# Separate PSUM banks and copies for the third x tile's transposes, and warm-up matmuls that read one broadcast column: a change to the first microseconds of an MLP forward and backward kernel

## The chip, the cores and the metric

The kernel runs on one core of one Trainium2 chip. The metric is the device time of one execution in microseconds (us). A profiled execution also has a span, from its first to its last traced instruction; for this kernel it is about 1.8 us shorter than the device time. Engines: PE is TensorE (PEld its weight loads), DVE is VectorE, ACT is ScalarE, POOL is GpSimd, SP is SyncE, which here only issues DMAs.

## The reference, cut to what matters

```python
def _fwd_reference(x, w1, w2):          # x [1, 2048, 640], w1 [640, 1536], w2 [1536, 640], bf16
    h = jax.nn.silu(jnp.einsum("bsd,df->bsf", x, w1))
    return jnp.einsum("bsf,fd->bsd", h, w2)

def reference(x, w1, w2, grad_out):     # the output and the three gradients
    _out, _vjp = jax.vjp(_fwd_reference, x, w1, w2)
    return (_out, *_vjp(grad_out))
```

These are six matrix products. The first product needs x with its 640 columns on partitions, that is, transposed. The rows are worked on in four chunks of 512.

## The kernel before: the opening

Only the opening of the first chunk is touched. TensorE is given 18 warm-up matmuls on a constant tile while the first inputs travel. Three x tiles of 128 rows are then transposed on TensorE, copied from PSUM to the tile `xT` by VectorE and ScalarE, and multiplied with w1, which comes in row blocks of 128 rows.

```python
NWARM = 18; NQ = 3; HC = NQ * P         # P = 128, DT = 640/128 = 5, FC = 512
NA = 8; FA = NA * P                     # eight output tiles are worked on at once
ps_h = tc.tile_pool(name="ps_h", bufs=8, space=PSUM)     # eight PSUM buffers, taken in turn
...
warm = cpool.tile([P, P], dt_in, name="warm")
early = [nc.vector.memset(warm[:], 1.0)]
wp = ps_h.tile([P, SC], FP32, name="wp", tag="hp")
for i in range(NWARM):
    early.append(nc.tensor.matmul(wp[:, 0:P], lhsT=warm[:], rhs=warm[:], start=True, stop=True))
...
early += [load_x(nc.sync, 0), load_x(nc.scalar, 1), load_x(nc.sync, 2)]
early += [load_w1(0, slice(0, FC), nc.scalar), load_w1(0, slice(FC, FA))]
early += [load_w1(k, slice(0, FA)) for k in range(1, 3)]
for k in range(3, DT):
    load_w1(k, slice(0, FA))
...                                     # later on the same queue: the rest of w1, then w2, ...
def pe_x(xT):
    slices = ((0, 1), (1, 3), (3, DT))
    tps = [ps_h.tile([P, hi - lo, NQ, P], dt_in, name="tp", tag="hp") for lo, hi in slices]
    for q in range(NQ):                 # x tile q
        for tp, (lo, hi) in zip(tps, slices):
            for dt_ in range(lo, hi):
                nc.tensor.transpose(
                    tp[:, dt_ - lo, q, :], x_nat[:, q, dt_ * P:(dt_ + 1) * P], ident[:])
    for k, (tp, (lo, hi)) in enumerate(zip(tps, slices)):
        copy_tp = nc.scalar.copy if k % 2 else nc.vector.tensor_copy
        copy_tp(out=xT[:, lo:hi, 0:HC], in_=tp[:].rearrange("p k q s -> p k (q s)"))

def h_first(xT, aT, ghT):
    pe_x(xT)
    ...
    for dt_ in range(DT):               # one row block of w1 after the other
        for ft in range(NA):
            mm(ft, dt_, slice(0, HC), dt_ == 0, False)   # 128x384 matmul on hs[ft]
    ...
```

Each PSUM tile `tp` holds columns of all three x tiles, so a copy can start only when the third tile has been transposed: in the profile before, the third tile's first transpose starts at 3.37 us and the first copy at 3.64.

## Time and profile before

| | before |
|---|---|
| device time, median of the 3 runs at hand (range) | 320.03 us (319.85 to 320.49) |
| span of the profiled execution | 317.7 us |
| PE busy | 313.2 us, 99% of the span |
| first matmul on w1's second row block | 5.60 us |

The profile's page gives the span, the busy time of each engine, and the chain of work that ended last, followed back from the last instruction.

```profile
span 317.7 us, 3605 instructions
...
PE 313.2 (99%) x1501; PEld 146.8 (46%) x1529; DVE 102.9 (32%) x182; ACT 77.2 (24%) x139; POOL 0.7 (0%) x6
...
PE 99%; issue 1%; DVE 0%; DVEq 0%
```

TensorE bounds the kernel. Time can be won only where TensorE waits or runs slowly, and that is the opening. The timeline of its first 6.3 us has the columns: start in us, duration of the merged group in us, engine, line, operation, tiles, shapes, count, and in brackets the idle time of the engine before it with what ended it.

```profile
0.29 0.17 DVE L158 MEMSET warm<- 128x128 bf16 x1 [0.29 <-issue]
...
0.51 2.10 PE L162 MATMUL wp<-warm 128*128 128x128 bf16 x18 [0.51 <-DVE warm L158]
...
2.43 1.39 PE L211 MATMUL tp<-ident,x_nat 128*128 128x128 bf16 x15
...
3.64 0.82 DVE L216 COPY xT<-tp 128x384 bf16<-128x384 bf16 x2 [3.19 <-PE tp L211]
...
3.75 0.80 ACT L216 COPY xT<-tp 128x768 bf16<-128x768 bf16 x1 [1.06 <-PE tp L211]
4.05 2.53 PE L251 MATMUL hp<-xT,w_nat 128*128 128x384 bf16 x13 [0.23 <-DVE xT L216]
...
4.86 0.44 PEld L251 LDWEIGHTS <-w_nat 128*128 128x128 bf16 x4 [0.39 <-DMA w_nat<-in_w_dram]
5.59 0.76 PEld L251 LDWEIGHTS <-w_nat 128*128 128x128 bf16 x6 [0.29 <-DMA w_nat<-in_w_dram]
```

Read from top to bottom: memset, 18 warm-ups, 15 transposes, copies, first h matmul at 4.05 us. The last two lines are weight loads that stood idle until a piece of w1 had landed. In the records of the single instructions the warm-ups are 105 to 108 ns apart (the first two 80), and so are the first transposes; from about 3.2 us the transposes are 55 to 57 ns apart, but for 62 and 66 where the third x tile arrives. Here this is called the clock of TensorE coming up, and the two paces half clock and full clock. The profile before has no record of the granted clock, so its moment is read from the spacing alone.

### The profile page before, as it was taken

The numbers are of one execution on the slowest core, as the hardware profiler recorded it, in microseconds if no ns is written. First come the engines' busy times: TensorE is split into PE (matmuls) and PEld (weight loads), VectorE is DVE, ScalarE is ACT, GpSimd is POOL, SyncE is SP. The second block draws the span as 40 slices with busy tenths as digits, with TensorE's granted clock in tenths as the row PEclk, the third lists the DMA queues.
The fourth block names the chain that finished last, engine by engine and source line by source line (L and its number), as shares of the span: only waits on it lengthen the run. The fifth ranks groups of instructions, "written<-read, shape, count | busy, mean of one in ns | idle before, by whom it ended". The sixth has DMA issues, their size and how long they took to land.

```text
span 317.7 us, 3605 instructions
## 1 busy us (share of the span) xinstructions
PE 313.2 (99%) x1501; PEld 146.8 (46%) x1529; DVE 102.9 (32%) x182; ACT 77.2 (24%) x139; POOL 0.7 (0%) x6
## 2 busy tenths in 40 slices
PE   9999999999999999999999999999999999999997
PEld 6644444444444444444444444444444444444444
DVE  1396631577310177700157741000000100001001
ACT  2592000654101354311064420111100001001110
POOL 0000000000000000000000000000000000000000
DMA  8989999999989885482644089919999999996011
GB/s 266 329 167 207 229 267 245 337 255 279 292 220 339 203 241 133 148 283 85 165 119 131 0 274 264 206 31 295 244 254 254 253 218 343 242 274 207 33 35 50
DMA packets 147264, 66.85 MB, mean 210 GB/s; under 512 B 113328, under 2 KB 146736, under 8 KB 147248
## 3 DMA queue, kind: packets, MB, share of 16 engines
q1 hardware_dynamic: 146960, 66.33, 82.0%
q10 hardware_dynamic: 288, 0.30, 0.3%
q8 instruction: 12, 0.20, 0.3%
q14 instruction: 4, 0.03, 0.0%
HBM read 9.18 MB, written 28.97 MB: 120 GB/s over the span
## 4 chain that ended last, share of the span: by engine, by line
PE 99%; issue 1%; DVE 0%; DVEq 0%
PE hp L299 32%; PE hp L283 16%; PE hp L388 16%; PE hp L439 15%; PE hp L220 13%; PE hp L251 3%; PE hp L419 1%; PE wp L162 1%; PE tp L211 0%; DVE xT L216 0%; DVE g L430 0%; DVE warm L158 0%; DVEq L430 0%; DVEq L467 0%
## 5 line engine op out<-in xcount | busy, mean ns | idle before, releaser
L283 PE MATMUL hp<-goT,w2T 128*128 128x512 bf16 x238 | 56.8, 380 | 0.1
L299 PE MATMUL hp<-aT,w_nat 128*128 128x512 bf16 x235 | 52.2, 379 | 0.3
L299 PE MATMUL hp<-ghT,w1T 128*128 128x512 bf16 x236 | 52.2, 379 | 0.2
L388 PE MATMUL hp<-a_blk,go_nat 128*128 128x512 bf16 x235 | 51.7, 379 | 0.3
L439 PE MATMUL hp<-gh_blk,x_nat 128*128 128x512 bf16 x220 | 48.3, 379 | 0.2
L220 PE MATMUL hp<-xT,w_nat 128*128 128x512 bf16 x192 | 47.8, 379 | 0.4
L307 ACT ACTIVATE oT<-hp 128x512 bf16<-128x512 f32 x24 | 14.4, 598 | 104.3 <-PE hp L299 104.3
L229 ACT ACTIVATE aT<-hp 128x512 bf16<-128x512 f32 x48 | 28.5, 614 | 37.2 <-PE hp L220 30.4
L283 PEld LDWEIGHTS <-w2T 128*128 128x128 bf16 x240 | 23.5, 98 | 28.3
L299 PEld LDWEIGHTS <-w_nat 128*128 128x128 bf16 x240 | 23.5, 98 | 28.3
L388 PEld LDWEIGHTS <-go_nat 128*128 128x128 bf16 x240 | 23.5, 98 | 28.3
L299 PEld LDWEIGHTS <-w1T 128*128 128x128 bf16 x240 | 23.4, 98 | 28.4
L290 DVE SCALAR_TENSOR_TENSOR ghT<-ghT,hp 128x512 bf16<-128x512 bf16 x48 | 32.5, 682 | 7.0 <-PE hp L283 7.0
L439 PEld LDWEIGHTS <-x_nat 128*128 128x128 bf16 x224 | 21.9, 98 | 26.5
L309 DVE CAST oT<-hp 128x512 bf16<-128x512 f32 x16 | 11.0, 690 | 70.6 <-PE hp L299 70.6
L236 DVE SCALAR_TENSOR_TENSOR ghT<-aT,v 128x512 bf16<-128x512 bf16 x48 | 32.6, 686 | 0.3
L220 PEld LDWEIGHTS <-w_nat 128*128 128x128 bf16 x200 | 19.5, 98 | 23.4
L235 DVE TENSOR_SCALAR v<-t 128x512 bf16<-128x512 f32 x48 | 20.1, 425 | 28.1 <-ACT t L233 28.1
L233 ACT ACTIVATE t<-hp 128x512 f32<-128x512 f32 x44 | 26.5, 620 | 0.0
L450 DVE CAST g<-hp 128x512 bf16<-128x512 f32 x7 | 4.8, 691 | 47.0 <-PE hp L439 28.2
L398 DVE CAST g2T<-hp 128x512 bf16<-128x512 f32 x7 | 4.8, 692 | 46.1 <-PE hp L388 46.1
L396 ACT ACTIVATE g2T<-hp 128x512 bf16<-128x512 f32 x8 | 4.8, 597 | 47.0 <-PE hp L388 47.0
(24 smaller groups left out, 42.0 us busy)
## 6 DMA issues: line engine op xcount, KB each, us to landing
aT_scr<-aT SPq DMA_DIRECT2D x4, 1536.0 KB, 6.2
ghT_scr<-ghT SPq DMA_DIRECT2D x4, 1536.0 KB, 8.0
out_dram<-o_sb SPq DMA_DIRECT2D x8, 640.0 KB, 3.7
oT_scr<-oT SPq DMA_DIRECT2D x4, 640.0 KB, 3.9
go_nat<-in_grad_out_dram SPq DMA_DIRECT2D x4, 640.0 KB, 7.7
gxT_scr<-oT SPq DMA_DIRECT2D x4, 640.0 KB, 5.2
w_nat<-in_w_dram SPq DMA_DIRECT2D x1, 1920.0 KB, 11.8
x_nat<-in_x_dram SPq DMA_DIRECT2D x3, 640.0 KB, 7.4
```

Source lines behind the costliest of these rows:

```text
L220: nc.tensor.matmul(hp[:], lhsT=w1_nat[:, dt_, ft * P:(ft + 1) * P], rhs=xT[:, dt_, :], start=(dt_ == 0), stop=(dt_ == DT - 1),)
L229: nc.scalar.activation(aT[:, ft, :], hp[:], ACT.Silu)
L233: nc.scalar.activation(t[:], hp[:], ACT.Tanh, scale=0.5)
L235: nc.vector.tensor_scalar(out=v[:], in0=t[:], scalar1=-0.5, scalar2=0.5, op0=ALU.mult, op1=ALU.add)
L236: nc.vector.scalar_tensor_tensor(out=ghT[:, ft, :], in0=aT[:, ft, :], scalar=1.0, in1=v[:], op0=ALU.subtract, op1=ALU.mult)
L283: nc.tensor.matmul(gp[:], lhsT=w2T[:, dt_, ft * P:(ft + 1) * P], rhs=goT[:, dt_, :], start=(dt_ == 0), stop=(dt_ == DT - 1),)
L290: nc.vector.scalar_tensor_tensor(out=ghT[:, ft, :], in0=ghT[:, ft, :], scalar=1.0, in1=gp[:], op0=ALU.add, op1=ALU.mult)
L299: nc.tensor.matmul(op_[:], lhsT=w_all[:, ft, dt_ * P:(dt_ + 1) * P], rhs=rhs_all[:, ft, :], start=(ft == 0), stop=(ft == FT - 1),)
L307: nc.scalar.activation(oT[:, dt_, :], op_[:], ACT.Copy)
L309: nc.vector.tensor_copy(out=oT[:, dt_, :], in_=op_[:])
L388: nc.tensor.matmul(gp[:], lhsT=go_nat[:, st, dt_ * P:(dt_ + 1) * P], rhs=a_blk[:, st, :], start=(st == 0), stop=(st == ST - 1),)
L439: nc.tensor.matmul(gp[:], lhsT=x_nat[:, st, dt_ * P:(dt_ + 1) * P], rhs=gh_blk[:, st, :], start=(st == 0), stop=(st == ST - 1),)
```

## The change

The intent is to start the first h matmuls earlier. The first two x tiles get PSUM banks of their own, so that their copies run while the third is still being transposed, and only a 128-column copy remains between the third tile's first transpose and the first h matmul. The warm-ups read one column of ones, repeated with step zero, so that the memset ahead of them shrinks from 128 columns to 2; a 19th warm-up fills the time won.

```diff
-    NWARM = 18
+    NWARM = 19
...
-        warm = cpool.tile([P, P], dt_in, name="warm")
+        warm = cpool.tile([P, 2], dt_in, name="warm")
+        warm_pp = warm[:, 0:1].to_broadcast([P, P])
...
-            early.append(nc.tensor.matmul(wp[:, 0:P], lhsT=warm[:], rhs=warm[:], start=True, stop=True))
+            early.append(nc.tensor.matmul(wp[:, 0:P], lhsT=warm_pp, rhs=warm_pp, start=True, stop=True))
...
         def pe_x(xT):
-            slices = ((0, 1), (1, 3), (3, DT))
-            tps = [ps_h.tile([P, hi - lo, NQ, P], dt_in, name="tp", tag="hp") for lo, hi in slices]
-            for q in range(NQ):
+            slices = ((0, 1), (1, DT))
+            for qs in ((0, 1), (2,)):
+                tps = [ps_h.tile([P, hi - lo, len(qs), P], dt_in, name="tp", tag="hp") for lo, hi in slices]
+                for k, q in enumerate(qs):
+                    for tp, (lo, hi) in zip(tps, slices):
+                        for dt_ in range(lo, hi):
+                            nc.tensor.transpose(
+                                tp[:, dt_ - lo, k, :], x_nat[:, q, dt_ * P:(dt_ + 1) * P], ident[:]
+                            )
                 for tp, (lo, hi) in zip(tps, slices):
-                    for dt_ in range(lo, hi):
-                        nc.tensor.transpose(
-                            tp[:, dt_ - lo, q, :], x_nat[:, q, dt_ * P:(dt_ + 1) * P], ident[:]
-                        )
-            for k, (tp, (lo, hi)) in enumerate(zip(tps, slices)):
-                copy_tp = nc.scalar.copy if k % 2 else nc.vector.tensor_copy
-                copy_tp(out=xT[:, lo:hi, 0:HC], in_=tp[:].rearrange("p k q s -> p k (q s)"))
+                    copy_tp = nc.scalar.copy if lo and len(qs) > 1 else nc.vector.tensor_copy
+                    copy_tp(
+                        out=xT[:, lo:hi, qs[0] * P:(qs[-1] + 1) * P], in_=tp[:].rearrange("p k q s -> p k (q s)")
+                    )
```

## The prediction

> **What bounds the kernel.** TensorE. Page: PE busy 313.2 of a 317.7 us span; chain of waits: 99% PE. From 5.60 us to the end the matmuls run back to back (longest start-to-start above the 216 ns pace: one of 431 ns at 13.5, about where a record is missing). Everything the change touches lies before 5.6 us, so the question is what ends last there.
>
> **The opening, from the timeline and the records of DMA landings.** The 128x128 memset runs 0.29 to 0.45 us (165 ns). Eighteen warm-up matmuls start at 0.51, 106 ns apart, the last at 2.29. Three x tiles land at 2.39, 2.82 and 3.33 us; each group of five transposes starts about 40 ns after its landing (2.43, 2.86, 3.37). So the transposes are bound by DMA, not by warm-ups. The third tile's first transpose releases the first VectorE copy (3.64, 358 ns for 384 columns); the first h matmul starts at 4.05. Four h matmuls run, then PE waits for w1's first row block, second half: landed 4.82, matmul 4.87 (weight load idle 0.39). After four more it waits for w1's second row block: landed 5.55, matmul 5.60 (idle 0.29). Later blocks land at 6.2, 6.85, 7.5, always ahead of their matmuls.
>
> **What the change does.**
> - Memset 64 times smaller: 165 ns to perhaps 60 to 100 (128x1 memsets on another engine take 99). Warm-ups start 0.07 to 0.1 us earlier; one more costs 106 ns; they end at about 2.40 as before, just as x lands.
> - Broadcast operands: I expect 106 ns spacing to stay. [...]
> - Separate copies: from VectorE's 358 ns (384 columns) and 549 ns (768), about 167 + 0.5 per column (estimate). The 256-column copy is done by about 3.6, before the third tile's first transpose ends; the 128-column copy takes about 230 ns instead of 358. First h matmul at about 3.92 instead of 4.05. ScalarE's copy grows from 768 to 1024 columns, about 1.0 us, but starts about 0.2 earlier: ends near 4.6 as before. VectorE's last copy (512 columns, about 420 ns) ends near 4.3.
> - Instruction order elsewhere is the same, except that the third xT load is issued after the first oT store; it is needed near 108 us, with tens of us to spare.
>
> **On the critical path.** The 0.13 us are gained ahead of two waits for w1 that do not move. The first eight h matmuls finish early and wait longer (idle 0.7 becomes about 0.85 us). The second row block's matmul still starts at about 5.6, so the gain is nearly zero.
>
> The clock is the other route: [...] spacing 106 ns until about 3.15 us and 56 ns after. [...] that too ends before 5.6 us.
>
> **Prediction.** 319.95 us, 80% range 319.4 to 320.6 (the range of before's three runs is 0.64 us). Chances: faster by over 2% 0.005, within 2% 0.985, slower 0.01.
>
> **Signs.** Right: first warm-up at 0.40 to 0.45; first h matmul at 3.85 to 3.95; weight load idle on w1 longer by about 0.13; second row block's matmul at 5.5 to 5.7; span 317.4 to 318.0. Wrong: PE idle on w1 shrinks, or that matmul starts before 5.45.
>
> **What would make it wrong.** Zero-step operands that run slower: 19 warm-ups at twice 106 ns would end near 4.4 and cost up to 1.5 us. A clock that comes up after 5.6 us. w1 landings that shift by chance; they set the start.

The forecast came to 319.95 us, 0.08 below the 320.03 of the three runs at hand; it does not split the 0.08. Cut from it, where marked, are what it said of broadcast operands and of the clock without a trace or run to show it, and with that one term, for the clock, to which it gave no figure. ScalarE's "about 1.0 us" for 1024 columns is an estimate; the profile before has 598 to 620 ns for its operations on 512 columns in PSUM and 798 for the copy of 768, which continue to 976 to 998.

## The result, and the profile after

| | before | after |
|---|---|---|
| median of 6 runs (range) | 320.16 us (319.72 to 320.63) | 320.09 us (319.36 to 320.52) |
| ratio of the means of the fast runs, 95% interval | | 0.9995 (0.9978 to 1.0011) |
| span of the profiled execution | 317.7 us | 317.8 us |
| first matmul on w1's second row block | 5.60 us | 5.75 us |

A ratio here is the mean time of one kernel's fast runs over the mean of the other's fast runs of the same rounds, so it is not quite the ratio of the medians.

The page after, with the chain's shares:

```profile
span 317.8 us, 3636 instructions
...
PE 315.1 (99%) x1530; PEld 147.6 (46%) x1530; DVE 102.9 (32%) x183; ACT 77.4 (24%) x139; POOL 0.7 (0%) x6
...
PE 98%; DMA 1%; DVE 0%; issue 0%; DVEq 0%; SPq 0%
```

PE's busy time and count differ by 1.9 us and 29 matmuls mostly because the trace before lacks some matmul records; 1530 matmuls are the whole program after, and 1529 before. So nothing may be read from that difference. The timeline of the opening, in the same columns as before:

```profile
0.25 0.06 DVE L159 MEMSET warm<- 128x2 bf16 x1 [0.25 <-issue]
...
0.38 2.21 PE L163 MATMUL wp<-warm 128*128 128x128 bf16 x19 [0.38 <-DVE warm L159]
...
2.67 1.52 PEld L213 LDWEIGHTS <-x_nat 128*128 128x128 bf16 x15 [0.35 <-DMA x_nat<-in_x_dram]
2.67 1.78 PE L213 MATMUL tp<-ident,x_nat 128*128 128x128 bf16 x15
...
3.53 0.29 DVE L218 COPY xT<-tp 128x256 bf16<-128x256 bf16 x1 [3.22 <-PE tp L213]
3.96 1.01 ACT L218 COPY xT<-tp 128x1024 bf16<-128x1024 bf16 x1 [1.27 <-PE tp L213]
4.07 0.23 DVE L218 COPY xT<-tp 128x128 bf16<-128x128 bf16 x1 [0.24 <-PE tp L213]
...
4.34 9.00 PE L255 MATMUL hp<-xT,w_nat 128*128 128x384 bf16 x80
```

The parts are as designed: the memset takes 0.06 us, the warm-ups start at 0.38 instead of 0.51, and a 128-column copy of 225 ns precedes the first h matmul. Yet that matmul starts at 4.34 us, later than before, and the h matmuls then run in one unbroken group; no line here waits for w1. Two things differ that the change did not aim at. The first x tile landed at 2.63 us instead of 2.39. And after the first pair (82 ns) the transposes are 106 to 107 ns apart to the last one: the record of the granted clock has it at full speed only from 4.59 us, where before it was up at about 3.2. The chain of waits for the first 6.2 us of each kernel (columns: start, duration, what) says the same:

```profile
...
0.51 2.10 PE wp L162 x18
2.61 1.01 PE tp L211 x11
3.62 0.02 issue
3.64 0.37 DVE xT L216
4.01 0.04 issue
4.05 0.81 PE hp L251 x4
4.86 0.01 issue
4.87 1.39 PE hp L251 x7
```

```profile
...
0.09 2.54 DMA x_nat<-in_x_dram
2.63 0.04 issue
2.67 1.78 PE tp L213 x15
4.46 1.78 PE hp L255 x10
```

The first fence is before, the second after. Before, the chain runs through the VectorE copy; after, from the landing of x through slow transposes straight into the h matmuls. (Before, four h matmuls take 0.81 us until the next starts at 4.87, where four at 0.16 us are 0.65: a wait for w1 lies in that piece.)

One sum holds for both; below it is called the identity. The span less the start of the first matmul on w1's second row block is 317.681 - 5.598 = 312.083 us before and 317.819 - 5.747 = 312.072 us after. All that differs between the two executions lies ahead of that matmul. Whether its start, 0.15 us later, is due to the change or to the execution is the question for the experiments.

### The profile page after: what moved, and what is told of

The parts are those of the page before. It is cut to its first block, busy times and chain, and to the rows that moved or that the text cites. A ratio compares the mean times of both kernels' runs of the same rounds, so it can differ in the third digit from the quotient of the medians.

```text
span 317.8 us, 3636 instructions
## 1 busy us (share of the span) xinstructions
PE 315.1 (99%) x1530; PEld 147.6 (46%) x1530; DVE 102.9 (32%) x183; ACT 77.4 (24%) x139; POOL 0.7 (0%) x6
## 4 chain that ended last, share of the span: by engine, by line
PE 98%; DMA 1%; DVE 0%; issue 0%; DVEq 0%; SPq 0%
PE hp L303 33%; PE hp L392 16%; PE hp L287 16%; PE hp L443 15%; PE hp L224 14%; PE hp L255 3%; PE hp L423 1%; DMA x_nat<-in_x_dram 1%; PE tp L213 1%; DVE g L434 0%; DVEq L434 0%; SPq L471 0%
```

## The experiments

Theory A is that of the prediction: the landing of w1's second row block sets the start of that matmul, so what is won earlier is lost in waiting. Theory B: the moment when the clock rises differs from execution to execution and sets the start. Theory C: the changed kernel itself makes the clock late, because broadcast operands count for less or because of the idle time before the first transpose.

All twelve profiles are put together here, with the two above. Times are us from the start of each span. "Copies" tells which form of the copies the kernel has. Landings are the last of the 16 completion records of a DMA. "Ended by" says "landing" where the second row block's first matmul starts within 0.05 us of that block's landing, and "pace" where the eight h matmuls before it took until then. How much later the landing was than TensorE (the start of the eighth h matmul plus 0.16) differs much: 0.07 us in before, 0.04 in e7 and 0.02 in e9, but 0.34, 0.43 and 0.47 in e3, e4 and e10.

| profile | copies | x lands | clock rises | first h matmul | row block 2 lands | its first matmul | ended by | span less that |
|---|---|---|---|---|---|---|---|---|
| before | old | 2.39 | 3.2 (spacing) | 4.05 | 5.55 | 5.60 | landing | 312.08 |
| after | new | 2.63 | 4.59 | 4.34 | 5.55 | 5.75 | pace | 312.07 |
| e1, before again | old | 2.52 | 6.18 | 4.37 | 6.23 | 6.54 | pace | 312.07 |
| e2, after again | new | 2.50 | 5.54 | 4.22 | 5.94 | 6.15 | pace | 312.07 |
| e3, copies only | new | 2.67 | 4.02 | 4.39 | 5.97 | 6.02 | landing | 312.09 |
| e4, warm-ups only | old | 2.71 | 4.56 | 4.56 | 6.24 | 6.29 | landing | 312.09 |
| e5, before, no wait for w1 | old | 2.50 | 5.13 | 4.35 | (5.83) | 6.01 | pace | 312.08 |
| e6, after, no wait for w1 | new | 2.24 | 5.40 | 4.08 | (5.47) | 6.01 | pace | 312.08 |
| e7, after, row block 2 late | new | 2.65 | 6.57 | 4.66 | 6.88 | 6.93 | landing | 312.09 |
| e8, after, 60 warm-ups | new | 2.60 | 4.29 | 6.75 | 5.99 | 8.04 | pace | 312.07 |
| e9, before, 1 warm-up | old | 2.42 | 5.96 | 4.27 | 6.35 | 6.40 | landing | 312.52 |
| e10, after, block 2 on ScalarE's queue | new | 2.56 | 6.22 | 4.27 | 7.04 | 7.08 | landing | 312.09 |
| e11, after, 1 warm-up | new | 2.53 | 6.06 | 4.26 | 5.97 | 6.43 | pace | 312.08 |
| e12, before again | old | 2.57 | 5.82 | 4.48 | 5.42 | 6.43 | pace | 312.08 |

Outputs were correct in all runs but e5 and e6. e1, e8, e11 and e12 are single runs whose state is unknown; the others are fast, and the span identity holds for both. The interval beside a ratio is that of 95%.

### e1: the kernel before, unchanged

No edit.

> The kernel before, unchanged, for a second look at its opening. Identity to be tested: span = 312.08 us + start of the first h matmul that reads w1's second row block (before: 317.681 - 5.598 = 312.083; after: 317.819 - 5.747 = 312.072). Theory A (that start is set by the landing of w1's second row block, 5.55 us in both profiles): start within 0.06 us of that landing. Rival B (the execution's own clock rise sets it: 3.15 us in the profile before, 4.59 in the one after): the rise comes at another time here, between 3.0 and 4.8 us, although the kernel is the same; if it comes after 4 us, the transposes run 106 ns apart throughout, the first h matmul starts at 4.4 to 4.6, and nothing waits for the second row block, so the start is 5.8 to 5.95. Rival C (the changed kernel itself makes the clock late): the rise is at 3.0 to 3.3 us again.

Measured: 320.39 us, one run. The clock rose at 6.18 us although the kernel is the one that had it at 3.2. The timeline of this profile:

```profile
2.56 1.78 PE L211 MATMUL tp<-ident,x_nat 128*128 128x128 bf16 x15
...
4.37 2.17 PE L251 MATMUL hp<-xT,w_nat 128*128 128x384 bf16 x7
4.37 0.10 PEld L251 LDWEIGHTS <-w_nat 128*128 128x128 bf16 x1 [0.18 <-issue]
4.64 0.15 PEld L251 LDWEIGHTS <-w_nat 128*128 128x128 bf16 x1 [0.17 <-issue]
4.96 0.15 PEld L251 LDWEIGHTS <-w_nat 128*128 128x128 bf16 x1 [0.17 <-issue]
```

The fifteen transposes take 1.78 us, as in the profile after, against 1.39. The weight loads come 0.27 and then 0.32 us apart and wait for nothing but their turn ("issue"): 0.32 is the pace of a 384-column matmul at half clock, against 0.16 us at full clock. The second row block's matmul starts 0.31 us after its landing. The change is thus not needed for a late clock, against theory C, and here theory B holds: the same kernel opens in either way. The rise is later than the 3.0 to 4.8 us that were expected under B, and the start (6.54) later than the 5.8 to 5.95. The landing itself came 0.68 us later than in the profile before, so the clock accounts for only 0.26 of the 0.94 us between the two starts. The identity holds.

### e2: the changed kernel, unchanged

No edit.

> The changed kernel, unchanged, for a second look and a ratio of its own. All theories: ratio 0.998 to 1.001 of the kernel before. A: the start of the second row block follows its landing by 0.06 us wherever the clock is up by 4 us. B: the clock rise is anywhere from 2.9 to 4.8 us. C: it is at 4.4 us or later again.

Measured: 319.83 us, ratio 0.9992 (0.9978 to 1.0005). The clock rose at 5.54 us, 0.95 us later than in the other profile of the same kernel. The second row block landed at 5.94 and its matmul started at 6.15, held up by the slow matmuls before it. That is what B says, but 5.54 is later than B's range (2.9 to 4.8) and is also what C expected (4.4 or later), so this profile does not part the two. The clock was not up by 4 us, so A's condition was not met here.

### e3: the copies alone

```diff
-            slices = ((0, 1), (1, 3), (3, DT))
+            slices = ((0, 1), (1, DT))
...                                     # pe_x as after; NWARM = 18 and the full memset as before
```

> Old warm-ups (18, full memset), new banks and copies. First VectorE copy of the third tile 225 ns instead of 358. From the start of the third tile's first transpose to the first h matmul: 0.55 us with a clock that is up (before: 3.372 to 4.051 = 0.679), 0.63 with one that is not (after: 3.714 to 4.344). A: the second row block still starts at its landing, ratio 0.9985 to 1.0015. B: the same ratio, and the gain of 0.13 us is kept only where the clock is late.

Measured: 319.94 us, ratio 0.9995 (0.9982 to 1.0008). From the third tile's first transpose (3.756) to the first h matmul (4.388) it is 0.632 us, as expected for a clock that is not yet up. The clock rose at 4.02 us, the eight h matmuls took 162 ns each, and then TensorE waited. The chain of waits and the wait list of this kernel (waiter, releaser, total, times, longest):

```profile
...
1.47 4.50 DMA w_nat<-in_w_dram
5.97 0.05 issue
6.02 0.99 PE hp L254 x5
```

```profile
PEld L254 <- DMA w_nat<-in_w_dram: 0.6, 1, 0.6
```

This is theory A as the prediction told it: with the clock up in time, the landing decides. The eighth matmul had started at 5.52 and took 0.16, so TensorE was ready at 5.68 and waited until 6.02. The copies' gain is inside that wait. The landing itself, however, is at 5.97 and not at 5.55.

### e4: the warm-ups alone

```diff
-    NWARM = 18
+    NWARM = 19
-        warm = cpool.tile([P, P], dt_in, name="warm")
+        warm = cpool.tile([P, 2], dt_in, name="warm")
+        warm_pp = warm[:, 0:1].to_broadcast([P, P])
...                                     # the matmuls read warm_pp; pe_x as before
```

> New warm-ups (19, 128x2 memset, broadcast column), old banks and copies. First warm-up at 0.38 us, last at 2.28, 106 to 107 ns apart. First h matmul 0.68 us after the start of the third tile's first transpose with a clock that is up, about 0.75 with a late one. A: ratio 0.9985 to 1.0015. B: the same, the clock rise scattered. C (broadcast operands do not count as work, or count less): the clock rise is at 4.4 us or later.

Measured: 320.16 us, ratio 1.0000 (0.9988 to 1.0013). First warm-up at 0.383 us, last at 2.277. From the third tile's first transpose to the first h matmul 0.763 us, against 0.632 in e3: the separate copies are worth 0.13 us at that point. The clock rose at 4.56 us, the row block landed at 6.24, and its matmul started at 6.29: landing again. A rise at 4.56 is within what C expected (4.4 or later); C is left to e8.

### e5 and e6: the wait for w1 taken away

The eight output tiles read the first 512 columns of w1's first row block for every row block. Their outputs are wrong, which doesn't matter for the times. Nothing is read before it has landed. The same edit in both kernels:

```diff
-                    lhsT=w1_nat[:, dt_, ft * P:(ft + 1) * P],
+                    lhsT=w1_nat[:, 0, (ft % 4) * P:(ft % 4 + 1) * P],
```

> The kernel before with the wait for w1 taken away: the eight output tiles of the first stage all read the first 512 columns of w1's first row block, which land first (wrong result on purpose). Theory A (landing of the second row block ends the opening where the clock is up): h matmuls run without a gap, so the second row block's first matmul starts 1.30 us after the first h matmul with the clock up (8 x 162 ns), up to 2.56 us with a clock that stays low (8 x 320), and no longer at a landing; about 5.35 to 5.9 us instead of 5.6 to 6.5. Span stays 312.08 us plus that start, within 0.03. Ratio 0.9980 to 1.0000. Rival (the landing doesn't matter, only clock and copies do): starts and ratio as without the edit, 0.9990 to 1.0010.

> The changed kernel with the same wait taken away (wrong result on purpose). A: what the copies gain is kept now: from the third tile's first transpose to the first h matmul 0.55 us (clock up) or 0.63 (clock low), against 0.68 or 0.76 in the run without the change, and the second row block starts 1.30 to 2.56 us after the first h matmul. Ratio about 0.0004 below that of the other kernel, which the times alone will not resolve; the profiles will.

Measured: before without the wait 319.93 us, ratio 1.0004 (0.9983 to 1.0026), one of its six runs at 321.87; after without the wait 319.98 us, ratio 0.9995 (0.9980 to 1.0010). The times tell nothing apart, as their intervals are wider than the effect. In the profiles the step from the third tile's first transpose to the first h matmul is 0.765 us in the old form and 0.630 in the new, at half clock in both. So the copies gain 0.135 us there.

The second row block's matmul starts at 6.01 us in both. With the new copies and transposes that started 0.16 us earlier, the first h matmul was 0.27 us earlier, but the clock rose 0.27 us later, at 5.40 instead of 5.13, and that undid it. Both profiles were of the kind where the pace decides, in which the wait that was taken away would not have been met: it does not show what the landing costs. As a test of theory A the pair is inconclusive.

### e7: the second row block late

```diff
-        early += [load_w1(k, slice(0, FA)) for k in range(1, 3)]
-        for k in range(3, DT):
+        early += [load_w1(k, slice(0, FA)) for k in (2, 3)]
+        for k in (1, 4):
             load_w1(k, slice(0, FA))
```

> The changed kernel with w1's second row block loaded in the place of the fourth (issued about 1 us later; results correct). A: its landing moves from 5.55 to 6.25 us to 6.8 to 7.7, the first matmul that reads it starts within 0.06 us of the landing whatever the clock does, span = 312.08 + that start (within 0.05), ratio 1.0025 to 1.0045. Rival (clock and copies end the opening): ratio 0.9985 to 1.0010.

Measured: 321.07 us, ratio 1.0040 (1.0021 to 1.0059), about 1.3 us. The block landed at 6.88 us and its matmul started 0.05 us later. The loads of weights in this profile:

```profile
6.55 0.11 PEld L255 LDWEIGHTS <-w_nat 128*128 128x128 bf16 x1 [0.17 <-issue]
6.93 1.09 PEld L255 LDWEIGHTS <-w_nat 128*128 128x128 bf16 x8 [0.26 <-DMA w_nat<-in_w_dram]
```

Over the six runs, when the landing is moved, time moves with it, as A says. The profile alone does not show it: the clock rose only at 6.57 us, and the first h matmul was itself held at 4.66 by the landing of the first half of w1's first row block at 4.61. By pace alone the matmul would have started at about 6.89 (the eighth h matmul at 6.728 plus 0.163), 0.04 us sooner. A landing and a late clock are that close together.

### e8: sixty warm-ups

`NWARM = 60` in the changed kernel.

> The changed kernel with 60 warm-ups, no gap from 0.38 us until the transposes. If broadcast operands run at full pace and count as work: spacing 106 to 107 ns, then 56 ns after a rise between 2.9 and 6.4 us; span = 312.08 + the start of the second row block, 7.5 to 9.0 us. If the gap of 0.25 to 0.48 us between the last warm-up and the first transpose is what makes the clock late (rival), the rise is at 3.0 to 3.3 us here. If broadcast operands don't count as work, all 60 stay 106 ns apart (to 6.7 us) and the clock rises after 6.7 us.

Measured: 321.88 us, one run. The warm-ups are 106 to 107 ns apart and then 58 to 60; the clock rose at 4.29 us, 3.91 us after the first of them, without any gap for TensorE to be idle in. The transposes that follow are 55 to 56 ns apart throughout. The tile's view gives minimum, median and maximum duration:

```profile
L163 PEld LDWEIGHTS <-warm x60: 98/151/151, 0.4 to 5.5; 128*128 128x128 bf16 x60
L163 PE MATMUL wp<-warm x60: 219/314/314, 0.4 to 5.6; 128*128 128x128 bf16 x60
```

Broadcast operands keep the pace at half clock (106 to 107 ns, as the old warm-ups' 105 to 108), and the clock rose at 4.29 us with nothing but such matmuls run before it. Their weight loads took 98 ns at the least and 151 in the median; those of the old warm-up tile took 150 to 152 at half clock in the profile before, and those of w1 and w2 97 to 98 from 5.6 us on. At full clock the warm-ups are about 3 ns further apart than the transposes (58 to 60 against 55 to 56); no profile has the old warm-ups at full clock, so whether the broadcast costs that is not shown. A rise at 4.29 without a gap shows that the gap is not needed to make the clock late. Neither form of theory C is needed, then, to explain a late clock; a small effect of either is not excluded by so few draws: with 18 old warm-ups the rise was at 3.2 to 6.2 us (five profiles), with the new ones (19, or 60 in e8) at 4.3 to 6.6 (seven). With a clock that is up, the new copies take 0.534 us from the third tile's first transpose to the first h matmul, against 0.679 in the profile before.

### e9 and e11: one warm-up

`NWARM = 1` in the kernel before (e9) and in the changed one (e11).

> The kernel before with one warm-up in place of 18, so that TensorE's steady work starts with the transposes at about 2.4 to 2.7 us and not at 0.5. In the ten looks so far the clock rose 2.6 to 6.2 us after the first warm-up. If the rise follows the start of steady work at a chance phase: it comes between 5.0 and 8.9 us here, the second row block starts at 6.3 to 7.2 us (all eight h matmuls before it mostly at 320 ns), some of its own eight and later ones run slow too, so that span is 312.08 + that start + up to 2 us; ratio 1.001 to 1.008. Rival (the rise is fixed by the kernel's start, warm-ups do nothing): rise 3.1 to 6.6 us, ratio 0.999 to 1.001.

> The changed kernel with one warm-up, for a second look at when the clock rises without them. The run with one warm-up before it had the rise at 5.96 us, which fits a chance phase after the start of steady work (5.0 to 8.9 us) and also the scatter seen with warm-ups (2.9 to 6.6). A rise after 6.6 us here speaks for the first; one before 5.0 for the second; between them it stays open. From the third tile's first transpose to the first h matmul 0.63 us, as the copies are the new ones. Span = 300.33 us + start of the first matmul that reads w2 (the same in the eleven profiles so far within 0.02).

Measured: e9 321.11 us, ratio 1.0035 (1.0019 to 1.0051), about 1.1 us; e11 320.27 us in a single run, 0.19 us above the one run beside it. The clock rose at 5.96 and 6.06 us, where both of the readings named beforehand allow it. That warm-ups help on average is shown by the ratio of e9; that they move the rise is not shown by these profiles. e11 and e12, one warm-up against eighteen, reached the second row block at 6.425 and 6.427 us, so in a single execution eighteen warm-ups can be worth nothing.

e9 is the one profile where the identity fails: 312.52 us instead of 312.08. A later wait explains the 0.44 us. The first matmul that reads w2 stood at 18.59 us behind w2's landing at 18.54:

```profile
18.58 1.41 PEld L299 LDWEIGHTS <-w_nat 128*128 128x128 bf16 x8 [0.75 <-DMA w_nat<-in_w_dram]
```

With that matmul as reference the identity holds again: the span less its start is 300.32 to 300.34 us in all fourteen profiles. In the others, w2 landed 0.07 to 2.6 us ahead of it: 0.27 and 0.30 in the two first profiles, 0.09 in e2, 0.07 in e3.

### e10: an attempt at a better version

```diff
-        early += [load_w1(k, slice(0, FA)) for k in range(1, 3)]
+        early += [load_w1(1, slice(0, FA), nc.scalar), load_w1(2, slice(0, FA))]
```

> An attempt at a better version: the changed kernel with the load of w1's second row block issued by ScalarE's queue before its table load, about 0.4 us earlier than on SP's queue (results correct). If the landing ends the opening in the executions with an early clock only: landing at 5.0 to 5.8 us instead of 5.5 to 6.2, ratio to the kernel before 0.9978 to 1.0003, nothing gained where the clock rises after 4.8 us. If DMA bandwidth and not the issue sets that landing: it stays at 5.5 to 6.2 us and the ratio is 0.9985 to 1.0010.

Measured: 320.72 us, ratio 1.0026 (1.0005 to 1.0047). Slower, and neither expectation was right. The block was issued at 1.10 us instead of 1.47 and landed at 7.04. The chain of waits:

```profile
...
1.10 5.93 DMA w_nat<-in_w_dram
7.04 0.05 issue
7.08 0.99 PE hp L255 x5
```

On one queue w1's row blocks land one after the other, 0.64 to 0.89 us apart (second to fourth, before, after and e1 to e4). Here the second and third, on two queues, landed 0.21 us apart, at 7.04 and 7.25, and the second half of the first row block landed at 5.69 us instead of 4.1 to 5.2 in the other profiles, so that TensorE waited for it until 5.73. That looks as if the three were served together, so that those needed first came late; this is inferred from these landings and was not tested further. No version was found that beats both kernels.

### e12: the kernel before, once more

No edit.

> The kernel before, unchanged, a third look. Clock rise anywhere from 2.9 to 6.6 us; start of the second row block = the later of its landing + 0.05 and of 1.3 to 2.6 us after the first h matmul; span = 312.08 us + that start within 0.03, unless the first matmul that reads w2 waits for w2's landing (slack 0.07 to 0.48 us in the other looks).

Measured: 320.28 us, one run. The clock rose at 5.82 us. The first h matmul was itself held by a landing, that of the first half of w1's first row block, at 4.43 us; the second row block had landed at 5.42, a full microsecond before its matmul at 6.43. In this execution the copies' gain would have been lost at the first h matmul already, as it was in e7.

## Why the prediction was right, and where it was not

- **The time.** 319.95 us was predicted with a range of 319.4 to 320.6; 320.09 was measured. That TensorE bounds the kernel is borne out; that the gain of about 0.13 us is absorbed before the steady part is seen in single profiles (e3, and e7 with its altered loads) and in no ratio. The number itself proves little: whether none or all of 0.13 us is kept, the time stays inside the range, and the profile after opened in another way than was told.
- **The costs of the parts.** Right. The copies measured 292, 225, 425 and 1012 ns against estimates of 295, 230, 420 and 1000; VectorE's five sizes in the two profiles, 225, 292, 358, 425 and 549 ns for 128, 256, 384, 512 and 768 columns, are about 160 ns plus 0.51 per column (a fit); the gain from the third tile's transpose to the first h matmul was 0.13 us as predicted (e3 against e4, e6 against e5). The memset took 60 ns and the warm-ups kept their spacing. The moments of the copies were not right: the last one was to end near 4.6 us and ended at 4.97, still 0.78 us ahead of the second row block's matmul, so the copies did not end the opening.
- **The step that failed:** "The 0.13 us are gained ahead of two waits for w1 that do not move." The landing of the second row block moved between 5.42 and 6.24 us over the profiles with the loads in their old order and at least 18 warm-ups. Of the seven profiles with the waits as in the two kernels (before, after, e1 to e4, e12), it ended the opening in three. In the other four TensorE arrived later than the data. The premise that x's landings bind the transposes failed with it: in the profile after, the third group started 0.26 us after its landing (3.71 and 3.46), because the ten before it ran at half clock (106 to 107 ns apart). Even in the profile before, the second group's first matmul followed at pace, at 2.94 us; the prediction's 2.86 is its weight load.
- **The second step that failed:** the clock's part "too ends before 5.6 us". One profile was taken for the rule. The rise was at 3.2 us in that one and at 4.0 to 6.6 us in the eleven others with at least 18 warm-ups, and in four of those seven profiles the start came after the data, behind slow transposes and h matmuls. The second row block's matmul started 0.15, 0.26 and 0.16 us later in after, e1 and e2 than its landing plus 0.05, and in e12 about 0.65 us later than with the clock up from the first h matmul (an estimate: 6.43 less 4.48 and eight times 0.162). The prediction took this to be over before it could count; each of the four is more than the change could gain. A clock that comes up after 5.6 us and landings that shift by chance did stand in its list of what would make it wrong.
- **The signs named beforehand.** The span was in its window. The first warm-up came a little sooner than its window (0.38 instead of 0.40 to 0.45). The first h matmul (4.34 instead of 3.85 to 3.95), the longer wait for w1 (none) and the start of the second row block (5.75 instead of 5.5 to 5.7) failed for the reasons just told and because x landed 0.24 us later. One of the two signs of being wrong came: TensorE's idle time on w1 shrank, from 0.39 and 0.29 us to none. e3, where the clock came in time, shows the wait that was foreseen.
- **Where the gain goes instead.** With a clock in time, into the wait for w1: all of it (e3). Where the first half of w1's first row block lands last (4.43 us in e12, 4.61 in e7), it is lost at the first h matmul. With a clock that rises among the eight h matmuls, about half is kept: starting 0.13 us earlier lets 0.13/0.32 more of a matmul run at the slow pace, each of which saves 0.16 us later, so 0.07 us. That half is an estimate from the two paces, not a measurement. Behind both stands w2, which in e2 and e3 landed 0.09 and 0.07 us before it was needed, so a gain much larger than 0.1 us would have met the next wait there.
- **Why no timing could show it.** The runs of the kernel before, unchanged, lie between 319.56 and 320.75 us. The identity explains the scatter where there is a profile: before, e12 and e1 reach the second row block at 5.60, 6.43 and 6.54 us and have spans of 317.7, 318.5 and 318.6. The effect of the change is a tenth of that.
- **Left open.** What sets the moment of the clock's rise was not tested. It came 2.7 to 6.2 us after the first warm-up in the twelve profiles with at least 18 warm-ups (at 3.2 to 6.6 us from the start of the span), and why it came when it did is not shown by any of them. In eleven of them TensorE stood idle for a few tenths of a microsecond at most on the way; e8, without a gap, had 3.91 us.

## What to carry to other kernels

Where the engine that bounds a kernel never stops after some point, find the first instruction of that steady part; the time is then a constant plus its start (here the span is 312.07 to 312.09 us plus it in thirteen of fourteen profiles), and a change ahead of it can be judged by that start in the profile, here to about 20 ns, while whole runs scatter by a microsecond. One profile of an opening shows one draw of landings and of the clock (which rose at 3.2, 6.18 and 5.82 us in three profiles of the kernel before): look at the same kernel two or three times before naming what bounds it. A copy shortened on a path that joins two other paths, here the data's arrival and the clock's rise, is worth what the slower of them leaves over.
